# Sparse attention and a rational MLP on one core: another set of planned transfer times, and other releases for the casts and loads

## The chip, the cores and the metric

The kernel runs on one core of one Trainium2 chip. The metric is the device time of one execution in microseconds (us). Three runs of the kernel before took 427.37, 423.12 and 430.69 us, so the median is 427.37 us. Engine names are those of the profile: PE (TensorE; its weight loads are PEld), DVE (VectorE), ACT (ScalarE), POOL (GpSimd), SP (SyncE). POOL and SP compute next to nothing here: they issue DMAs, each strictly in its own written order, and an instruction that waits holds up everything behind it on that engine.

## The reference, cut to what matters

```python
# q, k, v: (8 batches, 8 heads, 576 positions, 64), float32
scores = (q @ k.T) / 8                              # per batch and head
mask_local   = (0 <= i - j) & (i - j < 32)          # heads 0..3  ("L")
mask_strided = (i >= j) & (i % 32 == j % 32)        # heads 4..7  ("S")
attn = softmax(where(mask, scores, -1e9));  x = attn @ v      # -> x: (4608 tokens, 512)
h = x @ w_in                                        # (4608, 2048)
P = a0 + a1*h + a2*h*h + a3*h*h*h
Q = 1 + |b0|*|h| + |b1|*h*h
out = (P / (Q + 1e-6)) @ w_out                      # (4608, 512), float32
```

## The kernel before, in words

**Work.** The 4608 tokens are eight batches of 576 for the attention and nine chunks of 512 (`CH`) for the MLP. Chunk c can start when the attention of all batches that reach into it is done: chunk 2 needs batch 2, chunk 3 needs batch 3, and so on; chunks 7 and 8 both need batch 7.

**Attention of a batch** (`attention`) has four units in the order L0, S0, S2, L1, each of two heads. A unit is: mask and scores on PE (L791 and L800, or L876 and L884), row maximum on DVE (L810, L891), subtraction of the maximum on PE (L817, L898), exponential on ACT into `pL` or `pS` (L823, L904), a transpose of the probabilities into `ptL` or `ptS`, the product with v on PE (L853; L934 and L947), division on DVE (L862 and L864; L954 and L957). `turn` transposes the result on PE (L747, L754), and ACT copies it into `XT` (L770), the input of the MLP. In batches 0 and 1 the probabilities are transposed on PE; from batch 2 on (`NPE` = 2) a DMA transpose on SP does it (L841, L924).

**Input of a batch.** For batches 0 and 1, q and k are loaded straight into SBUF (tiles `h`, L563) and transposed on PE. From batch 2 on there are two steps. `casts(b)` issues, on POOL, five DRAM-to-DRAM DMAs that turn q, k (an L half and an S half each) and v into bf16 (L517), and two DMAs that load the strided half of v into `vS` (L572). `loads(b)` issues, on SP, four DMA transposes of q and k into `tq` and `tk` (L681, the L half first, then the S half), four copies that swap their partition halves (L692), and five loads of `vL` (L705, L709). `tq`, `tk`, `vL` and `vS` have two buffers each. `st["ops"]` holds the last `vL` load and the two `tk` transposes; `land[0..3]` are the probability transposes of the four units of the batch just issued.

**MLP of a chunk.** `mlp1(c)`: 64 matmuls (L982) in 16 groups of four, ACT copies each group to `h` (L988); two tiles `h` per chunk. On each tile DVE runs nine passes of 128x4096 (L1008, L1010, L1012, L1039, L1041, L1042, L1043, L1044, L1045), and ACT takes the logarithm and the exponential that make the reciprocal (L1036, L1038). I call such a round of nine passes a pade group; there are 18, the last one with another split. `mlp2(c)`: 64 matmuls (L1071), ACT copies to `os` (L1083), POOL stores (L1090; SP for the last chunk).

**What sets the order.** Every operation is registered with `P.op` under an engine, a planned duration, a key (lower goes first) and its dependencies; a DMA has a planned issue time and a planned transfer time `dma`. `Prog.schedule` then plays the program through once, at build time: it takes, on the engine that is free first, the ready operation of the lowest key, and the order that comes out is what each engine runs. At run time only this order and the semaphore waits are left; planned times no longer count. A DMA is planned to land at `dmafree[e] + 2.2`, where `dmafree[e]` adds the transfer times of the DMAs of that issuing engine, doubled while the other issuing engine's DMAs are still planned to be under way. The argument `after` adds dependencies which the data don't ask for; the issuing engine waits for them at run time too. Keys are `576*b + 144*unit` for attention, `576*b - 20` for loads, `512*c + 1500` and up for `mlp1`, `512*c + 2250` and up for `mlp2`. `Prog.filler` puts dummy matmuls (L136) where PE is planned to be idle near the start and in the last chunk, `0.75/0.216` of them per planned idle microsecond.

Of the kernel before, what the change touches and what calls it, by code (L numbers as in the profile page):

```python
# [84 lines left out]
class Prog:  # L85
# [65 lines left out]
    def schedule(self):  # L151
        for o in self.ops:
            o.ndep = len(o.deps)
            o.ready = 0.0
            for d in o.deps:
                d.users.append(o)
        pend = {e: [] for e in self.ENG}
        avail = {e: [] for e in self.ENG}
        free = {e: 5.0 if e == "pool" else 0.0 for e in self.ENG}
        order = self.order = {e: [] for e in self.ENG}  # L160
        dmafree = {e: 0.0 for e in self.ENG}
        for o in list(self.ops):
            if o.ndep == 0:
                heapq.heappush(pend[o.eng], (0.0, o.key, o.idx, o))
        left = len(self.ops)
        bank_free = [0.0] * 8
        bank_tile = [None] * 8
        held = [False] * 8
        nopen = {k: 0 for k in self.QUOTA}
        blocked = []  # L170

        def room(o, t):
            want = [p for p in o.pts if p.banks is None]
            if not want:
                return t
            if any(nopen[p.name] + 1 > self.QUOTA[p.name] for p in want):
                return None
            n = want[0].need
            assert len(want) == 1
            spots = [list(range(i, i + n)) for i in range(9 - n) if not any(held[i:i + n])]  # L180
            if not spots:
                return None
            if want[0].name in ("at", "ph") and 8 - sum(held) - n < 1 and nopen["po"] + nopen["sm"] < 1:
                return None
            when = [max(bank_free[i] for i in b) for b in spots]
            at = min(when)
            if at > t + 1e-9:
                return at
            spots = [b for b, w in zip(spots, when) if w <= t + 1e-9]

            def waste(b):
                if n == 2:
                    return b[0]
                return sum(1 for j in (b[0] - 1, b[0] + 1) if 0 <= j < 8 and not held[j]), -b[0]
            late = min(spots, key=waste)
            for p in want:
                p.banks = late
                nopen[p.name] += 1
                for i in p.banks:
                    held[i] = True  # L200
                    if bank_tile[i] is not None:
                        for d in bank_tile[i].ops:
                            o.deps[d] = 1
                    bank_tile[i] = p
            return t

        def close(o):
            for p in o.pts:
                p.left -= 1
                if p.left:  # L210
                    continue
                nopen[p.name] -= 1
                at = max(d.fin for d in p.ops) + 0.15
                for i in p.banks:
                    held[i] = False
                    bank_free[i] = at
                for q in blocked:
                    heapq.heappush(pend[q.eng], (q.ready, q.key, q.idx, q))
                blocked.clear()

        while left:
            best = None
            for e in self.ENG:
                if avail[e]:
                    t = free[e]
                elif pend[e]:
                    t = max(free[e], pend[e][0][0])
                else:
                    continue
                if best is None or t < best[0]:  # L230
                    best = (t, e)
            t, e = best
            while pend[e] and pend[e][0][0] <= t:
                _, k, i, o = heapq.heappop(pend[e])
                heapq.heappush(avail[e], (k, i, o))
            _, _, o = heapq.heappop(avail[e])
            at = room(o, t)
            if at is None:
                o.ready = max(o.ready, t)
                blocked.append(o)  # L240
                continue
            if at > t:
                heapq.heappush(pend[e], (at, o.key, o.idx, o))
                continue
            if e == "pe" and (o.key < -1000000000.0 or o.key >= (8 * 512 + 2250)) and t - free[e] > 0.5:
                spare = [i for i in range(8) if not held[i] and bank_free[i] <= free[e] + 0.2]
                if spare:
                    i = spare[-1]
                    n = int((t - free[e]) * 0.75 / 0.216) if free[e] > 0 else 0
                    if n:  # L250
                        bank_free[i] = max(bank_free[i], t)
                        f = self.filler(n, i, bank_tile[i], t)
                        if bank_tile[i] is None:
                            bank_tile[i] = PTile("fl", 1)
                            bank_tile[i].ops.append(f)
            free[e] = t + o.dur
            if o.dma is not None:
                at = max(dmafree[e], t + o.dur)
                busy = any(v > at for k, v in dmafree.items() if k != e)
                dmafree[e] = at + o.dma * (2 if busy else 1)  # L260
                o.fin = dmafree[e] + 2.2
            else:
                o.fin = t + o.dur
            order[e].append(o)
            left -= 1
            close(o)
            for u in o.users:
                lat = 0.0 if u.eng == o.eng else 0.15
                u.ready = max(u.ready, o.fin + lat)
                u.ndep -= 1  # L270
                if u.ndep == 0:
                    heapq.heappush(pend[u.eng], (u.ready, u.key, u.idx, u))
        self.order = order
        self.span = max(free.values())
# [95 lines left out]
def bass_strided_sparse_attn__then__act_rational_pade_kernel(nc, q, k, v, moe_w_in, moe_w_out, moe_a, moe_b, out):  # L370
# [143 lines left out]
    def bulk(s_t, d_t, b, h0, nh, hd, t, key, after):  # L514
        n = nh * S * D
        c = 1024
        P.op("pool", lambda e: e.dma_start(  # L517
            bass.AP(tensor=d_t, offset=(b * hd + h0) * S * D, ap=[[c, n // c], [1, c]]),
            bass.AP(tensor=s_t.tensor, offset=s_t.offset + (b * H + h0) * S * D, ap=[[c, n // c], [1, c]])),
            0.7, key, w=[t], dma=1.65 * nh / 4, after=after)  # L520

    vS_of = {}
    vL_of = {}
# [11 lines left out]
    def casts(b, after=None):  # L535
# [6 lines left out]
        for n in range(2):  # L542
            if b < NPE and n:
# [2 lines left out]
                VB = v.offset + b * H * S * D  # L546
                P.op("pool", lambda e: e.dma_start(
                    vl.t[:, 0, :, 0:64], bass.AP(tensor=v.tensor, offset=VB, ap=[[D, KW], [S * D, HL], [1, D]])),
                    0.8, key, w=[vt], dma=0.8, after=vl.prev)
                for h in range(HL):  # L550
                    P.op("pool", lambda e, h=h: e.dma_start(
                        vl.t[:, 1:NQ, h, 0:64],
                        bass.AP(tensor=v.tensor, offset=VB + (h * S + STRIDE) * D,
                                ap=[[D, KW], [64 * D, NQ - 1], [1, D]])),
                        1.1, key, w=[vt], dma=1.6, after=vl.prev)
            if b < NPE:
                h = stage[b, n] = R_h.next()
                hv = h.t[:, :, :].rearrange("p g c -> p (g c)")
            for i, (s_t, d_t, t) in enumerate(((q, q16, T_q[b][n]), (k, k16, T_k[b][n]))):
                if b >= NPE:  # L560
# [3 lines left out]
                    hv[0:TP, i * HL * TW:(i + 1) * HL * TW].rearrange("p (h c) -> p h c", c=TW),  # L564
                    bass.AP(tensor=s_t.tensor, offset=s_t.offset + (b * H + HL * n) * S * D,
                            ap=[[TW, TP], [S * D, HL], [1, TW]])),
                    0.8, key, w=[t], dma=2.0, after=list(after[3 * n + i]) + h.prev)
            if n == 0 and b >= NPE:
                bulk(v, vs, b, 0, HL, HL, T_v[b], key, after[2])
        vS = vS_of[b] = R_vS.next()  # L570
        for x in range(2):
# [1 line left out]
                vS.t[64 * x:64 * x + SB, :, :, :].rearrange("t h g d -> t h (g d)"),  # L573
                bass.AP(tensor=v.tensor, offset=v.offset + ((b * H + HL) * S + 8 * x) * D,
                        ap=[[16 * D, SB], [S * D, HL], [1, 8 * D]])),
                0.9, key, w=[vS], dma=2.0, after=after[5 + x])

    def weights_in():
        FH = Fmid // 2
        for i in range(2):  # L580
            T_win[i].new()
            for kk in range(NK1):
                P.op("pool", lambda e, kk=kk, i=i: e.dma_start(
                    Win[:, kk, FH * i:FH * i + FH], w_in[kk * 128:(kk + 1) * 128, FH * i:FH * i + FH]),
                     0.8, -9e4, w=[T_win[i]], dma=1.4)

    def weights_out(after=()):
        T_wout.new()
        for j in range(4):
            P.op("pool", lambda e, j=j: e.dma_start(  # L590
                Wout[:, 4 * j:4 * j + 4, :],
                w_out[512 * j:512 * j + 512, :].rearrange("(a p) n -> p a n", p=128)),
                0.8, -4e4, w=[T_wout], dma=3.3, after=after)


    NB = SC // TP
# [502 lines left out]
    for b in range(B):  # L1099
# [2 lines left out]
        if b == 0:  # L1102
            casts(NPE)
        if b == NPE:
            g = [cur["ops"]] * 3 + [[land[0]]] * 2 + [[land[1]]] * 2
            casts(b + 1, g)
        if NPE <= b + 1 < B:
            st = loads(b + 1, pace=land if b >= NPE else None)
        if b >= NPE and b + 2 < B:
            casts(b + 2, [[land[i]] for i in ((1, 2, 2, 3, 3, 3, 3) if b == NPE else (0, 0, 1, 2, 2, 3, 3))])  # L1110
        while nxt < NCH and (nxt + 1) * CH <= (b + 1) * S:
            gr, early = mlp1(nxt)
            if b + 1 < NPE:
# [46 lines left out]
```

## Time and profile before

| what | value |
|---|---|
| median of three runs | 427.37 us (423.12 to 430.69) |
| the profiled execution | 427.88 us, of it 426.1 us span |
| PE busy | 376.9 us (88% of the span) |
| DVE busy | 359.2 us (84%) |
| ACT busy | 291.9 us (69%) |
| POOL busy | 70.7 us (17%) |
| granted PE clock, mean | 0.948 |
| DMA moved | 47.48 MB |

The span runs from the first to the last instruction on the core. "Busy" is the sum of the instructions' durations; PE's instructions are pipelined and their ends modelled, so that a busy PE may still have room. The granted clock is given as a share of full speed. In lists of waits the columns are: the waiting engine with its tile and line, the one that released it, the sum of the waits in us, their number, and the longest one.

### The profile page before, as it was taken

What the parts mean: (1) busy time and instruction counts of PE and PEld (TensorE: products, weight loads), DVE (VectorE), ACT (ScalarE), POOL (GpSimd) and SP (SyncE); (2) the same over time, 40 slices, a digit from 0 to 9 for tenths busy, and PEclk for the clock granted to TensorE, in tenths of its full rate; (3) what the DMA queues carried; (4) which work ended last, traced back from release to release, by engine and by line L of the source; (5) the groups of instructions that cost most, each with busy time, mean ns of one, the idle gap of its engine ahead of it and who ended that gap; (6) DMA issues with size and microseconds to landing.
All of it is one profiled execution on the core that took longest, in us unless ns stands there. A gap on an engine that the chain in (4) does not pass through costs nothing.

```text
span 426.1 us, 8697 instructions
## 1 busy us (share of the span) xinstructions
PE 376.9 (88%) x3842; PEld 190.8 (45%) x3842; DVE 359.2 (84%) x315; ACT 291.9 (69%) x316; POOL 70.7 (17%) x112
## 2 busy tenths in 40 slices
PE   2777959989978598999998899989989999999796
PEld 2353536435534354554544355545444443344242
DVE  3471699999996128989999988999999999999992
ACT  2253795679465057778676848798587987989971
POOL 8951001001330012121030102000200200101100
PEclk9996996999975799899999989999999999999999
DMA  9999999106999999999699935901310110200202
GB/s 105 186 187 192 223 153 144 29 2 114 189 184 136 131 205 145 156 233 148 128 224 152 114 57 141 196 2 51 100 31 2 57 43 25 75 2 0 100 0 98
DMA packets 101830, 47.48 MB, mean 111 GB/s; under 512 B 89280, under 2 KB 97728, under 8 KB 101312
## 3 DMA queue, kind: packets, MB, share of 16 engines
q0 software_dynamic: 20384, 27.05, 36.4%
q1 hardware_dynamic: 81408, 19.87, 30.2%
q8 instruction: 30, 0.49, 0.5%
q14 instruction: 8, 0.07, 0.0%
HBM read 40.18 MB, written 18.28 MB: 137 GB/s over the span
## 4 chain that ended last, share of the span: by engine, by line
DVE 45%; PE 27%; ACT 10%; DMA 10%; issue 5%; SPq 3%; DVEq 0%; POOLq 0%
PE PSUM L982 9%; PE PSUM L1071 8%; DVE u L1012 6%; DVE h L1045 5%; DVE z L1043 5%; DVE u L1010 4%; ACT u L1036 4%; DMA ptS<-pS 4%; DVE z L1008 3%; DVE z L1041 3%; DVE xS L957 3%; DVE z L1042 3%; DVE z L1039 3%; ACT u L1038 3%; DVE z L1044 3%
## 5 line engine op out<-in xcount | busy, mean ns | idle before, releaser
L982 PE MATMUL PSUM<-XT,Win 128*128 128x512 bf16 x576 | 141.3, 393 | 4.0 <-ACT h L988 2.6
L1071 PE MATMUL PSUM<-Wout,h 128*128 128x512 bf16 x576 | 136.5, 388 | 6.3 <-DVE h L1045 4.0
L988 ACT ACTIVATE h<-PSUM 128x512 bf16<-128x512 f32 x144 | 83.0, 602 | 42.9 <-PE PSUM L982 42.9
L1071 PEld LDWEIGHTS PSUM<-Wout,h 128*128 128x128 bf16 x576 | 55.5, 99 | 73.2 <-DVE h L1045 3.8
L982 PEld LDWEIGHTS PSUM<-XT,Win 128*128 128x128 bf16 x576 | 54.0, 101 | 73.8 <-ACT h L988 11.4
L1036 ACT ACTIVATE u<-u,consts 128x4096 bf16<-128x4096 bf16 x17 | 63.1, 3710 | 15.2 <-DVE u L1012 15.2
L1038 ACT ACTIVATE u<-u 128x4096 bf16<-128x4096 bf16 x17 | 61.5, 3619 | 0.4
L1090 POOL DMA_DIRECT2D out_dram<-os x32 | 21.9, 686 | 179.6 <-ACT os L1083 179.6
L1012 DVE TENSOR_TENSOR u<-u,z 128x4096 bf16<-128x4096 bf16 x18 | 41.2, 2292 | 0.5
L1043 DVE TENSOR_TENSOR z<-z,h 128x4096 bf16<-128x4096 bf16 x17 | 39.0, 2291 | 0.5
L1041 DVE TENSOR_TENSOR z<-z,h 128x4096 bf16<-128x4096 bf16 x17 | 38.9, 2290 | 0.5
L1045 DVE TENSOR_TENSOR h<-z,u 128x4096 bf16<-128x4096 bf16 x17 | 38.9, 2286 | 0.4
L1083 ACT ACTIVATE os<-PSUM 128x512 f32<-128x512 f32 x34 | 19.2, 600 | 18.4 <-PE PSUM L1071 18.4
L1008 DVE TENSOR_SCALAR z<-h 128x4096 uint16<-128x4096 uint16 x17 | 20.6, 1213 | 12.7 <-ACT h L988 12.7
L770 ACT ACTIVATE XT<-PSUM 128x576 bf16<-128x576 bf16 (+2 forms) x40 | 19.8, 556 | 11.4 <-PE PSUM L754 8.8
L517 POOL DMA_DIRECT2D q<-in_q_dram x12 | 7.3, 610 | 110.2 <-DMA ptL<-pL 70.9
L891 DVE TENSOR_REDUCE ng<-PSUM 100x16 bf16<-100x576 f32 x16 | 11.9, 751 | 15.8 <-PE PSUM L884 15.8
L1010 DVE TENSOR_SCALAR u<-z,coef 128x4096 bf16<-128x4096 bf16 x18 | 24.1, 1338 | 0.4
L823 ACT ACTIVATE pL<-PSUM 128x960 bf16<-128x960 f32 x16 | 15.5, 966 | 12.2 <-PE PSUM L817 12.2
L1039 DVE TENSOR_SCALAR z<-h,coef 128x4096 bf16<-128x4096 bf16 x17 | 22.9, 1345 | 0.5
L904 ACT ACTIVATE pS<-PSUM 100x576 bf16<-100x576 f32 x16 | 10.2, 646 | 18.2 <-PE PSUM L898 18.1
L1044 DVE TENSOR_SCALAR z<-z,coef 128x4096 bf16<-128x4096 bf16 x17 | 21.8, 1284 | 0.5
(80 smaller groups left out, 394.0 us busy)
## 6 DMA issues: line engine op xcount, KB each, us to landing
out_dram<-os POOLq DMA_DIRECT2D x32, 256.0 KB, 3.2
q<-in_q_dram POOLq DMA_DIRECT2D x12, 288.0 KB, 6.2
k<-in_k_dram POOLq DMA_DIRECT2D x12, 288.0 KB, 7.7
vS<-in_v_dram POOLq DMA_DIRECT2D x16, 144.0 KB, 9.2
vL<-v SPq DMA_DIRECT2D x24, 96.0 KB, 6.1
Win<-in_moe_w_in_dram POOLq DMA_DIRECT2D x8, 256.0 KB, 12.7
Wout<-in_moe_w_out_dram POOLq DMA_DIRECT2D x4, 512.0 KB, 23.6
v<-in_v_dram POOLq DMA_DIRECT2D x6, 288.0 KB, 5.7
```

Of the source, the lines that this page charges most:

```text
L982: r = e.matmul(ph.f, Win[:, kk, f * 128:(f + 1) * 128], XT[:, kk, xc:xc + CH], start=(kk == 0), stop=(kk == NK1 - 1))
L988: P.op("act", lambda e, f=f, ph=ph, h=h: e.activation(h.t[:, f % G, :], ph.f, AF.Copy), 0.6, key, r=[ph], w=[h])
L1010: dv(lambda e, zz=zz, uu=uu: e.tensor_scalar(uu, zz, b1_ap, b0_ap, op0=Alu.mult, op1=Alu.add), ts + 0.28, r=[z, T_b], w=[u])
L1012: dv(lambda e, zz=zz, uu=uu: e.tensor_tensor(uu, uu, zz, op=Alu.mult), tt, r=[z], m=[u])
L1036: P.op("act", lambda e, uu=uu: e.activation(uu, uu, AF.Ln, bias=eps1, scale=1.0), 0.833 * W / 1000 + 0.28, key, r=[T_co], m=[u])
L1038: P.op("act", lambda e, uu=uu: e.activation(uu, uu, AF.Exp, scale=-1.0), 0.833 * W / 1000 + 0.19, key, m=[u])
L1039: dv(lambda e, zz=zz, hh=hh: e.tensor_scalar(zz, hh, a_ap[3], a_ap[2], op0=Alu.mult, op1=Alu.add), ts + 0.28, r=[h, T_co], m=[z])
L1041: dv(lambda e, zz=zz, hh=hh: e.tensor_tensor(zz, zz, hh, op=Alu.mult), tt, r=[h], m=[z])
L1043: dv(lambda e, zz=zz, hh=hh: e.tensor_tensor(zz, zz, hh, op=Alu.mult), tt, r=[h], m=[z])
L1044: dv(lambda e, zz=zz: e.tensor_scalar(zz, zz, a_ap[0], None, op0=Alu.add), ts + 0.22, m=[z])
L1045: dv(lambda e, zz=zz, hh=hh, uu=uu: e.tensor_tensor(hh, zz, uu, op=Alu.mult), tt, r=[z, u], m=[h])
L1071: r = e.matmul(po.f, h.t[:, j, m * 128:(m + 1) * 128], Wout[:, kk, :], start=(kk == 0), stop=(kk == NF - 1))
```

## The change

Three things are changed.

1. **Planned costs of DMAs and of their issue.** The start of POOL (5.0 to 3.5), the issue times and the transfer times of nearly all DMAs that POOL issues get other, mostly smaller values. They enter the plan only.
2. **Planned landings.** A DMA whose planned issue is later than 12 us is planned to land 1.5 us later than before, and one later than 60 us, 9 us later. This too enters the plan only. The number of filler matmuls per planned idle microsecond is cut from 0.75/0.216 to 0.7/0.216.
3. **Dependencies.** All seven DMAs of `casts(3)` now wait for the loads of batch 2 (three of them did already; the others waited for probability transposes of batch 2). `casts(b + 2)` for b from 2 on waits for the loads of batch b + 1, where it waited for the probability transposes of batch b. `loads(b + 1)` has no `pace` any more, which tied it to the probability transposes of batch b.

```diff
-        free = {e: 5.0 if e == "pool" else 0.0 for e in self.ENG}
+        free = {e: 3.5 if e == "pool" else 0.0 for e in self.ENG}
...
-                    n = int((t - free[e]) * 0.75 / 0.216) if free[e] > 0 else 0
+                    n = int((t - free[e]) * 0.7 / 0.216) if free[e] > 0 else 0
...
                 dmafree[e] = at + o.dma * (2 if busy else 1)
-                o.fin = dmafree[e] + 2.2
+                o.fin = dmafree[e] + 2.2 + (9 if t > 60 else 1.5 if t > 12 else 0.0)
...
     bulk() [q, k, v to bf16, DRAM to DRAM]:
-            0.7, key, w=[t], dma=1.65 * nh / 4, after=after)
+            0.55, key, w=[t], dma=1.4 * nh / 4, after=after)
     casts(), v of batches 0 and 1 (one DMA, then four):
-                    0.8, key, w=[vt], dma=0.8, after=vl.prev)
+                    0.8, key, w=[vt], dma=0.6, after=vl.prev)
-                        1.1, key, w=[vt], dma=1.6, after=vl.prev)
+                        0.8, key, w=[vt], dma=0.95, after=vl.prev)
     casts(), q and k of batches 0 and 1:
-                    0.8, key, w=[t], dma=2.0, after=list(after[3 * n + i]) + h.prev)
+                    0.8, key, w=[t], dma=1.75, after=list(after[3 * n + i]) + h.prev)
     casts(), vS:
-                0.9, key, w=[vS], dma=2.0, after=after[5 + x])
+                0.7, key, w=[vS], dma=0.6, after=after[5 + x])
     weights_in():
-                     0.8, -9e4, w=[T_win[i]], dma=1.4)
+                     0.55, -9e4, w=[T_win[i]], dma=1.2)
     weights_out():
-                0.8, -4e4, w=[T_wout], dma=3.3, after=after)
+                0.75, -4e4, w=[T_wout], dma=2.55, after=after)
...
         if b == NPE:
-            g = [cur["ops"]] * 3 + [[land[0]]] * 2 + [[land[1]]] * 2
+            g = [cur["ops"]] * 7
             casts(b + 1, g)
         if NPE <= b + 1 < B:
-            st = loads(b + 1, pace=land if b >= NPE else None)
+            st = loads(b + 1)
         if b >= NPE and b + 2 < B:
-            casts(b + 2, [[land[i]] for i in ((1, 2, 2, 3, 3, 3, 3) if b == NPE else (0, 0, 1, 2, 2, 3, 3))])
+            casts(b + 2, [st["ops"]] * 7)
```

## The prediction

> **What bounds the kernel now.** I read the busy times and slices first, then the waits of DVE, then windows around the gap they show.
>
> ```profile
> PE 376.9 (88%) x3842; PEld 190.8 (45%) x3842; DVE 359.2 (84%) x315; ACT 291.9 (69%) x316; POOL 70.7 (17%) x112
> DVE  3471699999996128989999988999999999999992
> PEclk9996996999975799899999989999999999999999
> DMA  9999999106999999999699935901310110200202
> ```
>
> One digit is 10.65 us. DVE is full from the sixth slice to the last but one, with one hole, slices 13 to 15 (128 to 160 us), where the granted PE clock falls too. So DVE sets the pace, except at the start, in the hole and in the tail. The same in windows (columns: stretch, its length, then busy us and count of PE, PEld, DVE, ACT and POOL, PE clock, DMA share, GB/s):
>
> ```profile
> 46.00:129.00 83.00, 72.49 (x935) 39.56 (x932) 80.18 (x75) 59.31 (x63) 11.15 (x18) 0.92 0.77 127
> 129.00:186.00 57.00, 49.58 (x588) 26.33 (x587) 34.32 (x35) 31.05 (x46) 8.09 (x13) 0.84 1.07 168
> 186.00:310.00 124.00, 117.88 (x1298) 60.14 (x1296) 119.22 (x99) 92.31 (x102) 15.46 (x24) 0.99 0.68 122
> ```
>
> DVE's waits from 129 to 186 us, all for PE, add up to 22.4 us:
>
> ```profile
> DVE ng L891 <- PE PSUM L884: 14.7, 2, 10.0
> DVE rc L954 <- PE PSUM L934: 4.5, 1, 4.5
> DVE rc L862 <- PE PSUM L853: 1.8, 2, 1.2
> DVE ng L810 <- PE PSUM L800: 1.2, 1, 1.2
> DVE xS L957 <- PE PSUM L947: 0.2, 1, 0.2
> ```
>
> From 46 to 412 us they are 27.1 us, so 4.7 us lie elsewhere: 0.9 of it at 123 us, 3.4 between 186 and 310. For the longest wait I looked at PE, SP and the DMA issues:
>
> ```profile
> 143.12 0.43 PE L876 MATMUL PSUM<-MS,IDN 128*128 128x288 bf16 x2 [5.16 <-issue]
> 123.59 1.30 SPq L681 DMA_TRANSPOSE tq<-q  x1
> 124.94 4.88 SPq L681 DMA_TRANSPOSE tk<-k  x1
> 129.86 13.43 SPq L841 DMA_TRANSPOSE ptL<-pL  x2
> tk<-k SPq DMA_TRANSPOSE x1, 18.1
> k<-in_k_dram POOLq DMA_DIRECT2D x1, 288.0 KB, 15.6
> ```
>
> PE stands at L876, the first strided scores of batch 3, and starts 0.1 us after the k transpose landed (124.9 + 18.1 = 143.0). That transpose took 18.1 us, where batch 2's took 4.6 us. It was issued late, held back by `pace` until the third unit of batch 2 had its probabilities, and it met the casts of batch 4, issued at 123.2 to 127.8 us (15.6 us to land; 3.9 to 5.8 us when alone at 70.8). DVE has spent chunks 0 and 1 by then; batch 3, which PE has in front of the rest of chunk 2, is not in. The attention comes too late, by its releases and by its place in PE's order.
>
> **The change part by part.**
>
> *Planned transfers (POOL's start, issue and transfer times).* They move places in the order, nothing at run time. For q's first cast of batch 2 the old costs give: issue done at 5.8; 19.2 each for batches 0 and 1; 11.2 for Win; 13.2 for Wout; 1.65 and 2.2 to land: 72.5 us. The new ones: 4.3, twice 12.6, 9.6, 10.2, 1.4, 2.2 and 1.5: 54.4 us. The trace has it issued at 24.4 and landed 27.1 us later: 51.5 us. For the k half that lands last: 79.1 planned before, 60.0 now, 58.7 in the trace. So the plan believed batch 2's inputs 20 us later than they came, and now has them 1 to 3 us late. By the same sum its loads are planned to end at about 77 us, with the allowance, against 91 before; in the trace they had landed at 71 us, yet PE took the first score of batch 2 only at 91.8 us. It should now come 14 to 18 us earlier.
>
> *The start.* PE had the S-half transposes of batch 0 at 20.5 us, though the trace lands those halves at 16.4 and 18.5 us (6.7 + 9.7 and 7.4 + 11.1); planned landings fall from 21.2 and 23.2 to 16.2 and 17.9. The S chain ended the start (divisions 30.1 to 34.0, then XT, MLP at 36.2). The second transpose can move forward by 22.15 - 18.5 = 3.6 us at most. If PE stands for the second S half with L's subtraction (L817, 17.87 us) behind it, up to 1.5 us are lost. I take -1.5, nearer the gain, since both halves have landed 0.6 us after that subtraction began.
>
> *The releases.* POOL: `casts(3)` now goes as one block when batch 2's loads have landed (72 us; its first three did at 70.8, the next two at 100.4, q and k of batch 4 from 111.5). SP: `loads(3)` no longer waits for batch 2's probabilities (100.2 and 123.6 us) but for its casts alone, at about 77 us; `tq`, `tk` of that ring slot were last read in batch 1, by 65 us. `casts(4)` cannot start before `loads(3)` is in, so the meeting that cost 18.1 us is excluded. Every wait added is on POOL; behind it stand stores (four `os` buffers, one chunk of slack, about 40 us) and the next casts. vS additionally waits for batch b-2's product, as before. Batch 3's loads thus end near 95 us instead of 143 us, and DVE needs chunk 3 only after chunk 2. The 22.4 us of waits should fall to the rate of the later batches, 3.4 us for four, or 1.1 us each on the generous side: for batches 2 and 3, 2.2 us remain. Bounds: at best nothing remains; at worst all 22.4 us.
>
> *The allowance of 9 us.* At run time nothing; in the order, a unit's products stand 9 us of other PE work later. With a lead over DVE that is free. At batch 2 the lead is thin: first score planned at 77, four units with 14.4 us from issue to planned landing end near 115 us, chunk 2's first matmuls take 7 us more, and DVE runs out of chunk 1 at 46.3 + 4 x 15.6 + 2 x 9.1 = 127 us (15.6 us is a pade group, 9.1 us one batch's attention, both by the means of the DVE rows). About 5 us are spare. Bounds 0 and +9; I take +2. Stores and loads under the same allowance have other work in front of them.
>
> *Fillers.* 42 filler matmuls become about 39. The 15 in the tail hold nothing up: L1071 starts at 415.00 us, 0.05 after DVE's L1031 gave its piece. One fewer is 0.2 us at most either way; I take 0.
>
> **Sum**, against the profiled 427.9 us (span 426.1): -1.5 - 22.4 + 2.2 + 2 = 408.2 us. The profiled run is 0.5 us above the median, so about 408 us in either measure. DVE is late next: the floor without any of the 27.1 us is 400.8, or 399.3 with the better start.
>
> *A word on the clock.* After the hole, matmuls of 512 columns start 0.43 us apart (133.1 to 134.0 us), against 0.22 us in the full stretches; the clock row reads 0.84 from 129 to 186 us. The Trainium skill, "TensorE: Matmul & The Clock Gate", Part 1, says the array falls to half clock after an idle window of some 3.4 us and needs as long a busy one to recover. By that rule the hole costs PE time beyond its own length, and closing it gives PE about 0.16 x 57 = 9 us of clock back; the sum, bound by DVE, stays at 408 without it.
>
> **The rivals.**
>
> *PE becomes the bound.* From 46 to 403 us PE is busy 327.6 of 357 us. Without DVE's 27.1 us the stretch would be 330 us, 99% of it PE. For it: attention now crowds into the earlier chunks, where PE carries both. Against: that busy time holds the lowered clock (0.92 and 0.84 in the first two windows). In its calm stretch, 275 to 400 us, PE is busy 120.4 of 125 us, 96%. At that share 327.6 us need 341: gain 16 us, **412 us**.
>
> *The probability transposes meet the casts instead.* The casts of b+1 start together when batch b's attention starts. Two `ptL` transposes that met casts took 10.9 us (129.9 us), against 3.0 alone: 7.9 us. If batches 2, 3 and 4, which have no lead yet, each pay that on the path, 23.7 us come back: **430 us**, no change. For it: DMA share 1.07 from 129 to 186 us. Against: PE's waits for these transposes, 46 to 412 us, are 2.6 and 1.9 us in all, and the new order holds the products back 9 us. The Trainium skill, "DMA: Bandwidth & Descriptors", section "Issuing engines are not separate DMA queues", says that all issuers run on the same 16 engines and interleave, which is this rival's rule; the trace's 10.9 against 3.0 agrees.
>
> *The serial chain is too slow.* Loads wait for casts, and the next casts for loads; nothing overlaps any more. Undisturbed, loads took 20 us (51.6 to 72) and the casts about 12: 32 us a batch. Disturbed, by rows of batches 3 and 4: casts 3.8 to issue and 15.6 to land, loads 12.4 and 19.4 us: 51 us. Batch 7's loads must be in by about 286 us (chunk 7's pade group, 355.9 us now, 22 earlier; less 7 for its matmuls and 41 for an attention like batch 2's). From 72 us that is 42.8 us a batch, the point from which it decides. At 51 us, five batches lose 8.4 each: **450 us**, slower. Against: the old disturbance came from overlaps the change removes.
>
> *The order is not what the costs say.* One greedy pass with PSUM quotas may place things otherwise; then the hole stays, 420 to 430 us. I count it with the no-change case.
>
> **How the numbers follow.** Forecast 0.48 (402 to 411), PE bound 0.18 (409 to 417), no change 0.21 (418 to 432), serial chain 0.13 (over 437). The predicted time is **408 us**. For 8 in 10 the range runs from 399 (the floor) to 427, into the no-change case. About 2% is what a measurement can tell here (three runs span 1.8%): faster means below 418.8 us, 0.66; within 0.21; slower 0.13.
>
> **What the changed profile would show.** Right: the first score of batch 2 (L791) by 80 us; SP's L681 for batch 3 at 77 to 85 us, landing within 10 us; no DVE wait over 3 us between 100 and 190 us; DVE full from 46 us on; PE clock near 1 from 129 us on. The start: MLP's first matmul at about 34.7 us. Wrong: DVE waits on L891 or L954 as before, with `ptL` or `ptS` over 10 us to land (casts in the way); L988 waiting for L982 with PE full (PE bound); or POOL's casts each released later than 43 us after the last (the chain).

## The result, and the profile after

The changed kernel took 408.4 us (median of four runs, 407.24 to 410.02). The kernel before, run beside it, took 426.69 us (423.12 to 430.69). The ratio is 0.960, with a 95% interval from 0.952 to 0.968: 18.3 us less. The profiled execution took 407.24 us with a span of 405.4, where the one before had 427.88 and 426.1, so the two traces lie 20.6 us apart. Here and below, a median is of all runs of a kernel, and a ratio with its interval leaves out the slow runs, those more than 1.5% above the fastest of the same kernel.

Busy times and slices of the changed kernel (one digit is now 10.1 us):

```profile
PE 364.2 (90%) x3838; PEld 184.0 (45%) x3838; DVE 358.8 (89%) x315; ACT 291.1 (72%) x316; POOL 72.6 (18%) x112
DVE  4571599999999899989996999999999999999981
PEclk9996999999999999999899999999999999999989
```

DVE does the same work (358.8 us against 359.2) and its hole at 128 to 160 us is gone. The clock row has lost its 7, 5 and 7 of about that place (slices 12 to 14). PE's busy time fell by 12.7 us although it lost only four matmuls. The windows (columns as before: stretch, length, busy us and count of PE, PEld, DVE, ACT, POOL, then PE clock, DMA share, GB/s):

```profile
43.00:128.00 85.00, 74.13 (x1068) 40.03 (x1066) 81.81 (x78) 64.52 (x74) 11.58 (x18) 1.00 0.87 149
128.00:184.00 56.00, 53.87 (x602) 27.34 (x603) 52.62 (x46) 40.62 (x50) 8.52 (x11) 1.00 0.90 160
184.00:308.00 124.00, 120.35 (x1321) 61.07 (x1320) 119.35 (x100) 94.34 (x102) 18.03 (x26) 0.99 0.62 116
```

In the middle stretch DVE is busy 52.6 of 56 us, where it was 34.3 of 57, and PE's clock reads 1.00 in place of 0.84. DVE's waits from 46 to 393 us:

```profile
DVE z L1008 <- ACT h L988: 14.2, 4, 12.3
DVE xS L957 <- PE PSUM L947: 1.7, 2, 1.5
DVE rc L954 <- PE PSUM L934: 1.1, 1, 1.1
DVE rc L862 <- PE PSUM L853: 0.9, 1, 0.9
DVE h L1045 <- ACT u L1038: 0.3, 1, 0.3
```

The longest, 12.3 us, began before 46 us and belongs to the start, as an equal one did in the trace before. With a wait of 0.2 us on L1020 the others add up to 6.1 us, against 27.1 before: 21.0 us less. L891, 15.8 us before, is not in the list. The timeline shows where the attention went (start, duration, engine, line, operation, tiles, count, and in brackets the idle time before it and its releaser):

```profile
70.89 0.63 POOL L517 DMA_DIRECT2D q<-in_q_dram  x1 [37.74 <-DMA tk<-k]
...
77.66 0.41 PE L876 MATMUL PSUM<-MS,IDN 128*128 128x288 bf16 x2
79.22 0.58 PE L791 MATMUL PSUM<-ML,IDN 128*128 128x480 bf16 x2
...
92.42 1.35 SPq L681 DMA_TRANSPOSE tq<-q  x1
93.81 1.44 SPq L681 DMA_TRANSPOSE tk<-k  x1
```

Batch 2's first scores start at 77.7 us (91.8 before). `casts(3)` goes at 70.9 us as a block, and batch 3's transposes follow at 92.4. Batch 3's first scores come at 116.2 us (123.8), its first strided ones too (143.1). From there batches start 37 to 41 us apart: 154.5, 191.4, 228.8, 270.1 us.

The 20.6 us between the traces: 1.0 at the start (DVE's first pade pass at 45.28, was 46.30), 21.0 of DVE's waits, and 2.0 lost in the tail, where the last wait of DVE grew from 4.32 to 6.28 us. These make 20.0; the other 0.6 us I have not placed.

### The profile page after: what moved, and what is told of

It is laid out like the page before. It is cut to its first block, busy times and chain, and to the rows that moved or that the text cites. A ratio compares the mean times of both kernels' runs of the same rounds, so it can differ in the third digit from the quotient of the medians.

```text
span 405.4 us, 8676 instructions
## 1 busy us (share of the span) xinstructions
PE 364.2 (90%) x3838; PEld 184.0 (45%) x3838; DVE 358.8 (89%) x315; ACT 291.1 (72%) x316; POOL 72.6 (18%) x112
## 4 chain that ended last, share of the span: by engine, by line
DVE 69%; PE 21%; ACT 5%; issue 3%; DMA 2%; DVEq 0%; POOLq 0%
DVE u L1012 9%; PE PSUM L1071 8%; DVE h L1045 8%; DVE z L1041 8%; DVE z L1043 7%; PE PSUM L982 7%; DVE u L1010 5%; DVE z L1039 5%; DVE z L1008 4%; DVE z L1044 4%; DVE z L1042 4%; DVE xS L957 4%; DVE xL L864 2%; DVE ng L810 2%; DVE ng L891 2%
## 5 line engine op out<-in xcount | busy, mean ns | idle before, releaser
L982 PE MATMUL PSUM<-XT,Win 128*128 128x512 bf16 x576 | 136.4, 384 | 4.4 <-ACT XT L770 1.7
L982 PEld LDWEIGHTS PSUM<-XT,Win 128*128 128x128 bf16 x576 | 52.2, 99 | 72.6 <-ACT h L988 11.7
L1090 POOL DMA_DIRECT2D out_dram<-os x32 | 20.6, 646 | 265.3 <-ACT os L1083 265.2
L1008 DVE TENSOR_SCALAR z<-h 128x4096 uint16<-128x4096 uint16 x17 | 20.8, 1221 | 14.2 <-ACT h L988 14.2
L957 DVE TENSOR_TENSOR xS<-PSUM,rc 100x512 bf16<-100x512 f32 x32 | 20.6, 685 | 3.0 <-PE PSUM L947 2.7
L1044 DVE TENSOR_SCALAR z<-z,coef 128x4096 bf16<-128x4096 bf16 x17 | 21.9, 1286 | 0.6
L1042 DVE TENSOR_SCALAR z<-z,coef 128x4096 bf16<-128x4096 bf16 x17 | 21.8, 1283 | 0.4
L810 DVE TENSOR_REDUCE ng<-PSUM 128x10 bf16<-128x960 f32 x16 | 18.3, 1150 | 2.7 <-PE PSUM L800 2.7
```

The source lines that it names most:

```text
L982: r = e.matmul(ph.f, Win[:, kk, f * 128:(f + 1) * 128], XT[:, kk, xc:xc + CH], start=(kk == 0), stop=(kk == NK1 - 1))
L1044: dv(lambda e, zz=zz: e.tensor_scalar(zz, zz, a_ap[0], None, op0=Alu.add), ts + 0.22, m=[z])
```

## The experiments

The account in the prediction was that the releases and the better times of batch 2 close the hole, and that the allowance is slack which costs 2 us. Its rivals were that one part alone does the work, and that the allowance is what does it. I took the change apart in three: the planned costs (part 1, with the filler factor), the allowance (part 2), the releases (part 3). The kernel before had a median of 433.46 us beside the first four runs, 427.39 beside the next four and 428.84 beside the last four; ratios are to the kernel before in the same rounds, with 95% intervals.

**The releases alone.** The kernel before, with part 3.

```diff
-            g = [cur["ops"]] * 3 + [[land[0]]] * 2 + [[land[1]]] * 2
+            g = [cur["ops"]] * 7
...
-            st = loads(b + 1, pace=land if b >= NPE else None)
+            st = loads(b + 1)
...
-            casts(b + 2, [[land[i]] for i in ((1, 2, 2, 3, 3, 3, 3) if b == NPE else (0, 0, 1, 2, 2, 3, 3))])
+            casts(b + 2, [st["ops"]] * 7)
```

> The kernel before with part 3 alone (releases of casts and loads); planned costs and landings as before. Theory A (attention is late both by its releases and by its place in PE's order): part of the 22.4 us between 129 and 186 us goes, because the casts of batch 4 can no longer meet the loads of batch 3 (18.1 us for one transpose), but batch 2 keeps its late place (24 of the 144 matmul groups of mlp1 ahead of its first score, as before; 20 in the changed kernel): 412 to 420 us. Rival B (only the meeting of casts and loads matters): all of the gain, 406 to 411 us. Rival C (only the planned order matters): no change, 423 to 430 us.

Measured: 432.23 us (427.41 to 437.35), ratio 0.993 [0.980, 1.007]: no change. The 412 to 420 us of the prediction's account and the 406 to 411 of the rival that gave the releases everything are both wrong; 423 to 430 is nearest. PE's and DVE's waits, 46 to 400 us (the profiled execution, 437.35 us, is the longest of its runs; the waits are read for their place), show that batch 3's loads no longer hold PE, and what does instead:

```profile
PE PSUM L934 <- DMA ptS<-pS: 14.8, 2, 11.5
PE PSUM L853 <- DMA ptL<-pL: 9.1, 2, 7.6
...
DVE rc L954 <- PE PSUM L934: 13.7, 3, 10.8
DVE rc L862 <- PE PSUM L853: 9.2, 4, 6.5
```

PE now stands at the products, for probability transposes that have not landed. The hole has changed its place.

**The planned costs alone.** The kernel before, with part 1 and the filler factor; its core:

```diff
-        free = {e: 5.0 if e == "pool" else 0.0 for e in self.ENG}
+        free = {e: 3.5 if e == "pool" else 0.0 for e in self.ENG}
...
-            0.7, key, w=[t], dma=1.65 * nh / 4, after=after)
+            0.55, key, w=[t], dma=1.4 * nh / 4, after=after)
```

> The kernel before with part 1 alone (planned transfer and issue times, POOL's start, the filler factor); landings without the allowance and the old releases. Its order has batch 2's first score after 14 matmul groups of mlp1 (20 in the changed kernel, 24 before), batch 3's after 29. Theory A: batch 2 comes in time, batch 3's loads still wait for batch 2's probabilities and meet the casts of batch 4, so a hole of about 10 us stays: 412 to 422 us. Rival C (order alone): 406 to 411 us. Rival D (without the allowance PE reaches transfers that have not landed and stands there, as before): 423 us or more, with PE waits on L791 or L876 that end with a landing.

Measured: 435.43 us (431.73 to 437.84), ratio 1.008 [0.998, 1.019]. The first scores of batch 2 do come earlier, at 72.3 us, but PE has waited 3.3 us for `tk` there, and again 5.0 us at 150.4; 9.2 us on the copies of `tk` at L791, 8.9 on `ptS` (46 to 400 us):

```profile
PE PSUM L791 <- DMA tk<-tk: 9.2, 3, 5.0
PE PSUM L934 <- DMA ptS<-pS: 8.9, 5, 3.8
```

This is what rival D had: 423 us or more, with PE standing at L791. The plan is nearer to the truth and leaves no room for being late.

**The allowance alone.** The kernel before, with this line:

```diff
-                o.fin = dmafree[e] + 2.2
+                o.fin = dmafree[e] + 2.2 + (9 if t > 60 else 1.5 if t > 12 else 0.0)
```

> The kernel before with part 2 alone (landings planned 1.5 and 9 us later), filler factor, costs and releases as before. Its order has batch 2's first score after 32 matmul groups of mlp1, that is after all of chunks 0 and 1. Theory A: DVE then runs out of chunk 1 before chunk 2 can start; an attention like batch 2's took 41 us and chunk 2's matmuls 7, against two pade groups of 15.6 us left: a hole of some 15 to 25 us in DVE on top of a partly closed old one, 430 to 445 us. Rival E (the allowance alone is what helps, because PE no longer stands at transfers): 405 to 415 us.

Measured: 495.7 us (491.48 to 498.15), ratio 1.148 [1.135, 1.160]. Slower was expected, but not by 62 us. DVE's waits, 46 to 400 us:

```profile
DVE z L1008 <- ACT h L988: 63.3, 6, 12.9
```

One is the start's 11.7 us; the others come once a chunk (12.9 us at 153.8, 10.2 at 208.2, 10.1 at 261.3, 8.5 at 309.7), for the first matmuls of a chunk whose batch is late. Batches 2 to 5 have their first scores at 97.5, 162.5, 214.3 and 268.3 us, 52 to 65 apart, where DVE's work is about 40 us a chunk (359 us over nine).

**All but the allowance.** The changed kernel, with the opposite of the last diff.

> The changed kernel without the allowance (costs and releases kept). Its order has batch 2's first score after 14 matmul groups of mlp1, batch 3's after 31, batch 4's after 32 (changed kernel: 20, 32, 48). Theory A: the loads come in time by the releases and the order is early; the allowance adds only slack, so 404 to 412 us. Rival D (PE then stands at transfers that have not landed): 415 to 430 us, with PE or DVE waits on L791, L876, L853 or L934 that end with a landing.

Measured: 438.09 us (433.05 to 448.18), ratio 1.011 [0.999, 1.024]. The prediction's account said 404 to 412, and falls here: without the step that it priced at +2 us the whole gain is gone. PE's waits from 46 to 400 us, and the timeline of one (the profiled execution is the longest of its runs; the waits are read for their place):

```profile
PE PSUM L853 <- DMA ptL<-pL: 24.6, 4, 10.1
PE PSUM L934 <- DMA ptS<-pS: 7.7, 4, 3.5
```

```profile
131.07 0.52 POOL L517 DMA_DIRECT2D q<-in_q_dram  x1 [1.57 <-DMA vL<-v]
...
134.24 13.74 SPq L841 DMA_TRANSPOSE ptL<-pL  x2
...
151.51 0.76 PE L853 MATMUL PSUM<-vL,ptL 96*64 96x65 bf16 x20 [8.88 <-DMA ptL<-pL]
```

Five casts of 288 KB are issued from 131.1 to 133.5 us, as soon as the loads ahead are in. The `ptL` transposes behind them, at 134.2, let PE stand 8.9 us. At 194 us the same: casts from 193.9, `ptL` at 194.3 takes 20.0 us to land, PE stands 10.1. The first scores of batches 2 to 7 come at 72.0, 111.0, 130.7, 187.6, 243.9 and 287.1 us, 20 to 57 us apart. In the changed kernel the first probability transpose follows the start of the casts by 5.0 us or more (154.4 and 159.4; 17, 8, 8 and 6 in the other batches), here by 3.2 and 0.4 in these two. The changed kernel's transposes still meet casts at times: `ptS` takes up to 10.4 us and `ptL` up to 8.0. PE does not wait for them there.

This is the rival "the probability transposes meet the casts", in the version without part 2. The Trainium skill, "DMA: Bandwidth & Descriptors", section "Issuing engines are not separate DMA queues", has it that transfers of all issuers share the same 16 engines; 20.0 us against 3.0 for a `ptL` alone agrees.

**All but the releases.** The changed kernel, with the old lines of part 3.

> The changed kernel with the old releases (costs and allowance kept). Its order has batch 3's first score after 46 matmul groups of mlp1, batch 4's after 58 (changed kernel: 32 and 48), since a planned landing that waits for a probability transpose now carries the 9 us twice. After the first two trials the theory is F: what counts is that PE is sent to a batch neither before its transfers are in nor after DVE has run out of the chunk before. By F, batch 3 is in place about 14 matmul groups late, close to one pade group: holes of some 12 us at each of batches 3 to 5, 435 to 455 us. Rival G (the allowance does it alone once the costs are right; releases are worth nothing): 406 to 412 us.

Measured: 476.62 us (469.68 to 478.14), against 427.39 before, a ratio of 1.115 by the medians. Worse than 435 to 455. DVE waits 53.8 us on L1008, the start's 12.3 among them. The first scores of batches 3 to 5 come at 144, 194 and 241 us, about 48 us apart after a gap of 65: too slow for DVE, as with the allowance alone. The reading that I give this is argued, not shown. With the old releases the planned chain of a batch runs through a probability transpose, the cast that waits for it and the paced load, and each adds its 9 us; with the new ones only casts and loads are in the chain.

**All but the planned costs.** The changed kernel, with the old figures of part 1.

> The changed kernel with the old planned costs (allowance and releases kept). Its order has batch 2's first score after 32 matmul groups of mlp1, as the trial with the allowance alone, then batch 3's after 33, batch 4's after 54. By F: a hole in DVE before chunk 2 of 15 to 25 us and smaller ones behind it, 425 to 445 us. Rival G' (costs are worth nothing beside allowance and releases): 406 to 412 us.

Measured: 423.04 us (421.01 to 425.83, ten runs), ratio 0.992 [0.989, 0.996], a little below the 425 to 445 of theory F and far above the 406 to 412 of its rival. Its slices:

```profile
DVE  3471699999994369899999999999989999999892
```

The hole sits in slices 13 to 15 (126 to 157 us; 10.5 us a slice), up to 149.9 us, when DVE's next pade group starts; behind it DVE is full. First scores come at 95.4 us for batch 2, and then at 136.4, 176.9, 214.1, 251.5: the even spacing of 37 to 41 us is there, but the row starts 18 us late. So what part 1 does beside the other two is to bring batch 2 forward. By the ratios (0.992 against 0.960) that is worth some 14 us.

**Which landings need the allowance.** The changed kernel with the 9 us on the probability transposes alone, and on all other landings alone:

```diff
-                o.fin = dmafree[e] + 2.2 + (9 if t > 60 else 1.5 if t > 12 else 0.0)
+                o.fin = dmafree[e] + 2.2 + (9 if t > 60 and o.dst.name[:2] == "pt" else 1.5 if t > 12 else 0.0)
```

(`!=` in the second.)

> The changed kernel, the 9 us given only to the probability transposes; all other landings after 12 us are planned 1.5 us late. Its order has batches 2, 3 and 4 after 15, 26 and 32 matmul groups of mlp1 (changed kernel: 20, 32, 48; without allowance 14, 31, 32), but each product with v stands 9 us later than its transpose. If the waits without the allowance came from PE standing at probability transposes behind casts (8.9 and 10.1 us on ptL there), these go: 408 to 418 us. If PE stands wherever it comes too early, loads take their place, with waits on L791 or L876 that end with a landing: 420 to 440 us.

> The changed kernel, the 9 us given to all landings after 60 us but those of the probability transposes (1.5 us there). Its order has the first scores of batches 2, 3 and 4 after 20, 33 and 48 matmul groups of mlp1, like the changed kernel (20, 32, 48), but the products follow their transposes closely. If PE's standing at the probability transposes is the price: waits on ptL and ptS of 3 to 10 us in each of batches 3 to 7, 418 to 435 us. If the place of the first scores alone counts: 406 to 413 us.

Measured: 419.99 us (416.24 to 420.52), ratio 0.981 [0.973, 0.989], and 404.67 us (403.49 to 407.21), ratio 0.948 [0.941, 0.955]. The first lies at the edge of the 420 to 440 of its second reading. There PE's waits for probability transposes are gone, as they should be, and loads have taken their place:

```profile
PE PSUM L876 <- DMA tk<-k: 6.5, 1, 6.5
...
PE PSUM L791 <- DMA tk<-tk: 3.6, 2, 3.0
```

The second comes out just below the 406 to 413 of the reading that the place of the first scores alone counts. PE waits for a DMA once from 46 to 400 us, though no product is held back by 9 us:

```profile
PE PSUM L934 <- DMA ptS<-pS: 0.4, 1, 0.4
```

Its first scores come at 76.8, 114.6, 152.6, 193.5 and 232.5 us and its casts at 70, 113, 153, 189 and 229: nearly the changed kernel's. So what counts is that the other landings, those of casts, loads and stores, are planned late. The batches are then evenly spaced, and the first probability transpose follows the start of the casts by 8 us or more. The longest landings shrink, and the medians don't tell the versions apart. For `ptL`, first without any allowance and then in this version:

```profile
DMA to landing us min/median/max: 3.0/4.5/20.0
DMA to landing us min/median/max: 3.5/4.8/6.1
```

The allowance between a transpose and its product, when it stands alone, brings the ratio from 1.011 to 0.981; beside the other it adds nothing.

**The order without the run-time wait.** The changed kernel's order, kept as it is, but with the casts' waits for the preceding loads taken out after the order is drawn (`SOFT` holds the casts from batch 2 on, each with its `after`; the lines that collect it are left out here, and they make the line numbers higher by 3):

```diff
     P.schedule()
+    for o, ds in SOFT:
+        for d in ds:
+            o.deps.pop(d, None)
```

> The changed kernel with its order kept instruction for instruction; only at run time the casts no longer wait for the loads of the batch before (the dependencies are taken away after the order is drawn). In the changed kernel's trace POOL waits for a landing only once, 37.7 us ahead of the casts of batch 3; the later casts go out behind a store without waiting. If part 3 acts through the drawn order alone (theory F): the casts of batch 3 go out at about 33 us, meet the loads of batch 2, and nothing behind it moves: 406 to 412 us. If the wait itself keeps transfers apart: the loads of batch 2 (4.5 us median for a transpose) take over 8 us, batch 2's first score stands and DVE gets a wait over 3 us near 77 to 130 us: 414 to 425 us.

Measured: 421.83 us (420.58 to 424.6), ratio 0.988 [0.982, 0.995], some 14 us above the changed kernel. The drawn order alone does not do it. The time lies in the 414 to 425 us of the second reading, but PE did not stand at batch 2's first score, as that reading had it; it stopped before. The whole difference comes from one place, where `casts(3)`, free of its wait, went at 33.2 us in the midst of the loads of the start. It took 37 to 40 us to land, and the first two of batch 2's transposes took 25 us (8 and 6 in the changed kernel). Behind that place the drawn order does hold: the first scores come at 93.3, 131.6, 169.9, 206.8 and 244.2 us, spaced as in the changed kernel. The later casts stand behind stores in POOL's order and never waited for a landing in the changed kernel either. PE's timeline around the gap:

```profile
66.77 0.12 PEld L838 LDWEIGHTS PSUM<-IDN,pL 128*96 128x96 bf16 x1 [1.56 <-ACT pL L826]
80.96 1.01 PEld L838 LDWEIGHTS PSUM<-IDN,pL 128*96 128x96 bf16 x9 [14.07 <-issue]
80.95 1.23 PE L838 MATMUL PSUM<-IDN,pL 128*96 128x128 bf16 x10 [15.64 <-issue]
```

PE stops after the first weight load of a group of ten, with "issue" as its reason: the profile shows no semaphore that holds it. That is read in the last section.

**The place in the order by keys.** The changed kernel without the allowance, and with the attention of batches 2 to 7 moved back by its key, by 750:

```diff
-        base = b * 576
+        base = b * 576 + (750 if b >= NPE else 0)
```

> The changed kernel without the allowance, as in the trial that took 438 us, but with 750 added to the attention keys of batches 2 to 7. The order then has the first scores of batches 2 to 7 after 16, 32, 48, 64, 80 and 96 matmul groups of mlp1 (changed kernel 20, 32, 48, 64, 80, 96; without allowance 14, 31, 32, 48, 64, 80). If the place of the attention in PE's order is what the allowance bought (theory F): 404 to 415 us, with the waits of L853 and L934 for ptL and ptS (24.6 and 7.7 us without the allowance) under 6 us together. If it bought slack between each transpose and its product (theory H): those waits stay, 425 to 440 us.

Measured: 504.37 us (499.79 to 512.84), ratio 1.181 [1.168, 1.193]. In PE's order the first scores stand behind 16, 32, 48, 64, 80 and 96 groups of `mlp1`, close to the changed kernel's 20, 32, 48, 64, 80 and 96 (counted at L791). But the key also puts `mlp2` ahead of attention that is ready. The largest sum among PE's waits, over the whole run (40.5 us of it from 46 to 400 us):

```profile
PE PSUM L1071 <- DVE h L1045: 54.2, 10, 10.3
```

PE stands at `mlp2` for DVE, with scores that could run behind it. From 46 to 400 us the waits for `ptL` and `ptS` fall from 32.3 to 8.4 us, as the place would nearly have it, but the time is far above both forecasts. The run doesn't answer the question: it has moved more than the place.

**The best two once more, side by side.** The changed kernel and the version with the allowance on all landings but the probability transposes, five rounds.

> The changed kernel once more, on the same chip and in the same rounds as the next one: 0.955 to 0.965 of the kernel before.

> The changed kernel with the allowance on all landings but those of the probability transposes, once more beside the changed kernel. If its 404.7 us was a gain over the changed kernel: about 0.948 of the kernel before and 3 to 4 us below the changed kernel. If it was the chip of that day: within 1.5 us of it.

Measured: 407.83 us (407.57 to 410.23), ratio 0.956 [0.951, 0.960], and 405.83 us (403.5 to 408.2), ratio 0.950 [0.944, 0.955]. The second, neither 3 to 4 us below nor within 1.5, has the lower median both times that it was run, by 2.0 us here, but the intervals overlap, and I don't call it settled. The tails, timeline of the last `mlp2` blocks in the changed kernel (its first trace) and then in this version (the trace of these five rounds):

```profile
384.24 8.75 PE L1071 MATMUL PSUM<-Wout,h 128*128 128x512 bf16 x32 [3.90 <-DVE h L1045]
392.83 1.67 PE L136 MATMUL PSUM<-FL 128*128 128x512 bf16 x7
394.34 7.07 PE L1071 MATMUL PSUM<-Wout,h 128*128 128x512 bf16 x32
```

```profile
387.63 5.13 PE L136 MATMUL PSUM<-FL 128*128 128x512 bf16 x23
394.04 7.08 PE L1071 MATMUL PSUM<-Wout,h 128*128 128x512 bf16 x32 [1.28 <-DVE h L1031]
```

In the changed kernel DVE has the piece that the last block needs at 392.3 us, but PE is in the `mlp2` block before it until 392.8 and then in seven fillers until 394.3: 2.0 us late. In the other version PE is done with its fillers early and starts 0.06 us after the piece (392.76 + 1.22). DVE's last wait is 6.28 us in the first (7.37 in the changed kernel's second trace) and 4.32 in the second. Part of it is given back: DVE there waits 1.7 us for ACT's L1004 a little earlier.

The fillers are not all of it. The 32 matmuls of the block ahead of them took 8.75 us, where the others here take 7.07 or 7.08, at a lower granted clock (windows of that block, first in the changed kernel, then in the other version; columns as before):

```profile
384.00:393.00 9.00, 8.76 (x33) 3.68 (x34) 8.61 (x7) 7.89 (x5) 0.00 (x0) 0.81 0.01 2
380.70:388.00 7.30, 7.27 (x34) 3.35 (x35) 5.64 (x3) 7.25 (x3) 0.00 (x0) 1.00 0.11 40
```

PE had stood for 3.9 us ahead of the slower block and for 2.7 us ahead of the other; no run tests whether that is why.

## Why the prediction was right, and where its reasons were not

The time came out as forecast, 408.4 against 408, and in part by luck: the hole cost 2.8 us less than the sum allowed, the start and the tail 2.5 us more, and the step on the allowance was wrong in kind. By its steps:

- **The bound and the hole: right.** The prediction had DVE's waits of 22.4 us at 129 to 186 go, with 2.2 to remain and 2 more for the allowance. In the corresponding stretch, 128 to 184 us, 2.7 us remain, and over the whole run 6.1, where the steps made it 4.7 + 2.2 + 2 = 8.9. The sum was 2.8 us too dear here.
- **The start: right in place, a little large.** 1.0 us in place of 1.5; the first matmul of the MLP comes at 35.1 us, not 34.7.
- **The fillers: mis-sized.** They were costed at nothing, within 0.2 us, and the tail lost 2.0. The step looked at the number of fillers and not at what they follow: in the new order the `mlp2` block ahead of them starts 8.1 us before DVE gives the last piece (384.24 and 392.3), where it had 11.4 us (403.52 and 414.95). Seven fillers of 1.5 us together then stand in the way; without them the last block would have been some 0.5 us late. That block ahead also ran 1.7 us longer than at a clock of 1.00; in the kernel before it ran long too (8.38 us), with time to spare.
- **The planned times: right in their effect.** Batch 2's scores at 77.7 us, 14.1 earlier (14 to 18 forecast). The run without this part puts some 14 us on it, beside the other two parts; alone it gained nothing.
- **The releases: half right.** `casts(3)` went as a block at 71 us (72 forecast) and batch 3's `tq` and `tk` landed within 2.2 to 4.2 us, as forecast. But `loads(3)` was forecast at 77 us and was issued at 92.4. The step counted the waits of the loads and not what stands ahead of them in SP's order, which are batch 2's probability transposes, issued from 87.8 to 92.4 us. It did no harm, since batch 3's scores begin at 116.
- **The allowance: wrong.** "At run time nothing" is true of the planned figure, and the step drew from it that the allowance only costs. Without it the ratio is 1.011 in place of 0.960. On the landings of casts, loads and stores it makes the planner space the batches evenly (37 to 41 us apart, 20 to 57 without it), and so decides when casts, loads and probability transposes are on the DMA engines together. The same steps without the allowance would have summed to 406 us, where 438 were measured (433 for the kernel before beside it).
- **"Attention now crowds into the earlier chunks": wrong.** Only batch 2 is drawn earlier, behind 20 groups of `mlp1` where it stood behind 24. From batch 4 on attention stands later in PE's order than before (48 groups against 45, 64 against 60, 80 against 68, 96 against 82, counted at L791). In time, the first scores of batches 4 and 5 are still earlier (154.5 and 191.4 us against 166.0 and 200.2), those of batches 6 and 7 are not (228.8 and 270.1 against 225.9 and 266.5).

The rivals. *PE as the bound*: not so as a whole, but for 10 us it is: from 213 to 223 us PE is busy without a gap at clock 1.00, and DVE waits 2.9 us there, the dip to 6 in its row of slices. PE's 12.7 us of busy time given back are above the 9 us that the clock rows promised, and the Trainium skill's rule on idle windows ("TensorE: Matmul & The Clock Gate", Part 1) agrees with a clock that reads 1.00 once the hole is shut. *The probability transposes meet the casts*: this is what the releases bring with them when they stand without the allowance, at 432 and 438 us; I had priced it at 430. Against it I had put that products are held back 9 us; the run with the allowance on all other landings shows that they need not be, since with the casts and loads planned late the meetings become rare. *The serial chain*: casts start 36 to 45 us apart (70.9, 115.8, 154.4, 190.2, 228.0), about at the 42.8 us from which it was to decide. It didn't, as the first and longest gap came with a lead, and the later casts waited for POOL's stores and not for landings. With the allowance and the old releases the first scores of batches 2 to 6 came 46 to 65 us apart, and there a chain seems to have decided, by the reading argued above.

What stays open: whether the casts could be held behind the probability transposes at run time in the order drawn without an allowance. That was not tried, since in that order SP has the loads of the next batch ahead of the last transposes (for batch 5 `tq` and `tk` at 148 to 154 us, for batch 4 `ptS` at 160.8 and 167.7), and the waits would close a circle. Also, no run separates the even spacing from the collisions that it avoids: the rows show both together.

## What to carry to other kernels

Where an order is drawn at build time from planned transfer times, exact times need not make a good plan: here, with nearly true costs and no allowance, PE stood at transposes that were late, and the gain came only once the landings of casts, loads and stores were planned 9 us late. Parts of such a change are not to be priced one by one: as ratios to the kernel before, the planned costs, the allowance and the releases gave 1.008, 1.148 and 0.993 alone, 1.011, 1.115 and 0.992 with the allowance, the releases or the costs left out, and 0.960 together. When you cost a moved load, read what stands ahead of it on its issuing engine, and when you cost a filler, read what it stands behind.

## What the runs showed of the hardware that was not expected

In the run without the casts' wait PE stood still for 14 us in the midst of a group of ten matmuls, with no semaphore wait that the profile shows. The DMA queues (queue and kind, packets, MB, and the time that their packets took as a share of 16 engines) from 66 to 78 us, and then from 78 to 80:

```profile
q1 hardware_dynamic: 1069, 0.27, 106.4%
q0 software_dynamic: 153, 0.46, 21.8%
```

```profile
q1 hardware_dynamic: 1474, 0.27, 71.5%
q0 software_dynamic: 262, 0.16, 53.0%
q8 instruction: 1, 0.02, 3.2%
```

From 58 to 78 us the queue q8, of kind "instruction", has no packet there, while in the changed kernel it has one from 58 to 66 and one from 66 to 78. The packet comes between 78 and 80 us, and PE goes on at 80.95. In the same 12 us the packets of q1, which carries SP's transposes and loads, are slow: 1.064 x 16 x 12 us over 1069 packets are 0.19 us each in the mean, against 0.016 from 78 to 80. I read this as instructions that came late while transfers crept. That PE's own code was in that packet is inferred from the times; and what slowed the transfers, whose engines moved only 60 GB/s then, is not shown.

The other figure is the price of meeting: a `ptL` transpose lands in 3.0 us alone, and took 20.0 us when issued 0.4 us behind the first of five casts of 288 KB, which themselves took 4.5 to 15.0. The small transfer came in last.
